# Counting the softmax sums out of bounds inside layer 1 of the last feed-forward group, with one relu of that layer put behind two PSUM copies of layer 2

## Chip, cores and metric

The kernel runs on one core of one Trainium2 chip. The metric is the device time of one execution in microseconds (us), here given as the median of several runs. Names used for the engines: PE or TensorE (matmuls; PEld is its loading of weights), DVE or VectorE, ACT or ScalarE, POOL or GpSimd, SP or SyncE (issues DMAs).

## The reference, cut to what matters

Attention over 8 batches and 8 heads (1152 keys, head size 64) with pairs of queries averaged, so that 576 rows of 512 values come out for each batch. Then a "mixture of depths": in each batch the 128 rows with the highest gate score go through a two-layer feed-forward network; the rest are passed on unchanged. All is float32.

```
    q_pool = q.reshape(B, H, S // factor, factor, D).mean(axis=3)
    scores = scale * np.matmul(q_pool, k.transpose(0, 1, 3, 2))
    scores = scores - np.max(scores, axis=-1, keepdims=True)
    attn = np.exp(scores)
    attn = attn / (np.sum(attn, axis=-1, keepdims=True) + 1e-09)
    return np.matmul(attn, v).astype(np.float32)
...
    scores = np.einsum('bsd,d->bs', x, w_gate)
    out = x.copy()
    for b in range(B):
        top_idx = np.argpartition(-scores[b], capacity)[:capacity]
        xe = x[b, top_idx]
        h = np.maximum(xe @ w1, 0.0)
        ye = h @ w2
        g = 1.0 / (1.0 + np.exp(-scores[b, top_idx]))
        out[b, top_idx] = x[b, top_idx] + g[:, None] * ye
```

w1 is 512 x 1024, w2 is 1024 x 512, and the capacity is 128.

## The kernel before, in words

**Attention.** `run` goes through 32 pairs of heads in halves. Of each half, TensorE makes the scores (L878), ScalarE their exponentials (L885) without the subtraction of a maximum, TensorE the product with the values (L896). Because no maximum is taken off, the kernel keeps all sums of exponentials in a tile `sums` (128 x 576) and at the end counts how many lie within fixed bounds (0.05 and 1e12). If any lies outside, a branch at the end of the program (label "again") computes everything anew in another way; with these inputs it isn't taken.

**Routing.** `routed` ranks the gate scores of a batch, fetches the chosen 128 rows with an indirect DMA (the tile `xe`, for the last batch a slice of a `v_sb` tile), and turns them for TensorE.

**Feed-forward.** The chosen rows are handled in two groups of four batches, in `ending`, after the attention. A matrix product is cut into quarters and made from seven products of quarters or of sums of quarters instead of eight (Strassen's scheme in Winograd's form). Sums of inputs come from `four_sums` (VectorE, L1410) or `input_sums` (GpSimd, L1256). Layer 1 of the second group (batches 4 to 7) is the generator `layer` within `split`. Of its seven products, four are whole (`first_product`, L1330, 16 matmul records each) and three are cut into seven smaller ones again (`inner_layer`, its matmuls at L1296, its first copy at L1308, its six other PSUM readers being VectorE sums at L1357, one product being read by two of them). `layer` ends each piece with a `yield`: 1 the product of a11 and b11; 2 an inner layer, the sum `rest(c11, u)` and `relu(c11)`; 3 the product of s2 and t2; 4 an inner layer; 5 the product of s1 and t1; 6 an inner layer, a sum for layer 2, and `rest(u, c22)` with its relu; 7 the product of s3 and t3, which two VectorE sums read, `relu(c22)`, three sums for layer 2, and last `rest(c21, v)` and `relu(c21)`. A `rest` is a VectorE sum of 128 x 1024 (L1357), a `relu` a ScalarE activation (L1490).

Layer 2 works on two batches at a time. Batches 4 and 5 use c11 and u (c12), batches 6 and 7 use c21 and c22. `second_of` makes the seven products of the first of these two in the order 1, 5, 2, 7, 3, 4, 6 (`second_product`, L1344, 8 matmul records each). ScalarE copies products 1, 5 and 3 out of PSUM (L1420, L1422, L1429), VectorE adds the others (L1357), scales by the gate and adds the row itself (`scaled`, L1352). The products of batches 6 and 7 are written out at the end of `ending` (copies at L1616 and L1618). Then four indirect scatters on GpSimd's queue (`written`, L1240) put the rows into the output in device memory.

**The count.** `counted` (L1644) reads `sums` twice on VectorE with an accumulated result, each pass followed by a read of the accumulator; `outside` adds over the partitions with a small matmul into a PSUM buffer (L1659), copies it (L1661), adds the two values (L1663) and turns them into an integer `count_i` (L1665). `values_load` (L1612) then loads that integer into a register on all five engines, with a branch hint (L1823), ahead of the branch (L1793).

**What sets the order.** The program is written in the order in which every engine's queue gets its instructions; nothing is reordered by a scheduler. `pieces(unit, n)` runs n pieces of a generator, and between them pieces of the routing (`waiting`) and of the weights' sums. Waits between engines follow from the tiles. The PSUM pool has four buffers of two banks, taken in turn by `banks()`: a product has to wait until the one four turns before it has been read.

Of the kernel before, what the change touches and what calls it, by code (L numbers as in the profile page):

```python
# [540 lines left out]
class _Plain:  # L541
# [814 lines left out]
    def add(self, to, x, y):  # L1356
        self.nc.vector.tensor_tensor(out=to, in0=x, in1=y, op=ALU.add)  # L1357
# [83 lines left out]
    def ending(self, halves, old):  # L1441
# [7 lines left out]
        def pieces(unit, n=None, of=1):  # L1449
            nonlocal done  # L1450
            for i, _ in enumerate(unit):
                for _ in range(of):
                    if done in behind:
                        next(waiting)
                    for _ in range(2):
                        next(weights, None)
                    done += 1
                if i + 1 == n:
                    break
# [10 lines left out]
        def halves_of(turned):  # L1470
            k = self.ND // 2
            return turned[:, :, 0:k, 0:w], turned[:, :, k:, 0:w]

        def first():
            a = [half_of for token in self.tokens[0 : self.B // 2 : 2] for half_of in halves_of(token["turned"])]
            c = [self.hidden_of(rooms[0][:, k * n : (k + 1) * n], w) for k in range(4)]
            m = [self.hidden_of(room[:, 4 * n : 5 * n], w) for room in rooms]
            return a, c, self.first_layer(a, inputs, c, m)

        def lines(room):  # L1480
            return self.lines_of(room)[:, :, 0:w]

        def across(room):
            return room.rearrange("p (t f) n -> p f t n", t=2)

        def rest(to, x):
            self.add(to, to, x)

        def relu(to):
            nc.scalar.activation(to, to, AF.Relu)  # L1490

        def split(a):
            u, v = (lines(room[:, 4 * n : 5 * n]) for room in rooms)
            c11, c21, c22 = (lines(rooms[1][:, k * n : (k + 1) * n]) for k in (0, 2, 3))
            c = [c11, u, c21, c22]
            temps = [
                [lines(rooms[0][:, k : k + half]) for k in range(2 * n + 3 * i * half, 2 * n + 3 * (i + 1) * half, half)]
                for i in range(2)
            ]
            two, six, seven = operands  # L1500
            s1, s2, s3, s4 = inputs
            t1, t2, t3, _ = (self.summed(1, i) for i in range(4))
            x, product, add = second(1, 0, c), self.first_product, self.add

            def layer():
                copy(across(u), product(a[0], self.quarter(1, 0, 0)))
                yield
                self.inner_layer(two, c11, temps[0])
                rest(c11, u)
                relu(c11)  # L1510
                yield
                add(across(v), across(u), product(s2, t2))
                yield
                self.inner_layer(seven, c21, temps[1])
                yield
                add(across(c22), across(v), product(s1, t1))
                yield
                self.inner_layer(six, u, temps[0])
                self.four_sums(*x[1:], slice(2, 3))
                rest(u, c22)  # L1520
                relu(u)
                yield
                ps = product(s3, t3)
                add(across(c22), across(c22), ps)
                add(across(v), across(v), ps)
                relu(c22)
                self.four_sums(*x[1:], slice(0, 2))
                self.four_sums(*x[1:], slice(3, 4))
                rest(c21, v)
                relu(c21)  # L1530
                yield

            return c, x, layer()

        def second(i, j, c):
            if i == 0:
                a = [c[2 * j + k][:, :, t, :] for t in range(2) for k in range(2)]
            else:
                a = [c[2 * j + k][:, 4 * t : 4 * t + 4, :] for t in range(2) for k in range(2)]
            s = self.lines_in(rooms[1 - i][:, 2 * j * n : 2 * (j + 1) * n], self.NFC // 2, w, 4)  # L1540
            return self.tokens[4 * i + 2 * j : 4 * i + 2 * j + 2], a, s
# [13 lines left out]
        a, c, layer = first()  # L1555
# [21 lines left out]
        x, y = second(0, 0, c), second(0, 1, c)  # L1577
        self.four_sums(*x[1:])
        pieces(layer, of=2)
        layer = self.second_of(*x, acc[1])  # L1580
# [3 lines left out]
        a = [half_of for token in self.tokens[self.B // 2 :: 2] for half_of in halves_of(token["turned"])]  # L1584
# [7 lines left out]
        self.input_sums(a, inputs, slice(3, 4))  # L1592
        self.inner_inputs(operands[1])
        self.input_sums(a, inputs, slice(2, 3))
        c, x, layer = split(a)
        pieces(layer)
        self.scattered(y[0])
        y = second(1, 1, c)
        layer = self.second_of(*x, acc[1])
        pieces(layer, 3)  # L1600
        low = self.counted()
        pieces(layer, 1)
        self.four_sums(*y[1:])
        pieces(layer, 1)
        outside = self.outside(low)
        pieces(layer)
        self.scattered(x[0])

# [218 lines left out]
```

## Time and profile before

| what | value |
|---|---|
| median of 3 runs | 674.19 us (674.08 to 674.79) |
| the profiled execution's own time | 673.19 us |
| its span, first to last instruction | 671.5 us |
| TensorE busy | 664.0 us, 99% of the span |
| mean granted TensorE clock | 0.997 |
| layer 1 of the second group begins on TensorE | 616.70 us (first whole product) |
| layer 2 of batches 4 and 5 begins | 639.92 us |
| the count's matmul (L1659) | 649.60 us |
| last scatter issued (L1240) | 666.65 us |

All times within the trace are counted from the start of the span. A row of the timeline gives the start, the time from the first start to the last end of a merged group, engine, line, operation, written and read tiles, shapes and number, and in brackets the idle time of the engine before it and what is thought to have ended it. Matmuls overlap, so the starts of following groups say more of TensorE's pace than their lengths do. A row of the table of stretches gives the length, then each engine's busy time and number of instructions.

### The profile page before, as it was taken

The numbers are of one execution on the slowest core, as the hardware profiler recorded it, in microseconds if no ns is written. First come the engines' busy times: TensorE is split into PE (matmuls) and PEld (weight loads), VectorE is DVE, ScalarE is ACT, GpSimd is POOL, SyncE is SP. The second block draws the span as 40 slices with busy tenths as digits, with TensorE's granted clock in tenths as the row PEclk, the third lists the DMA queues.
The fourth block names the chain that finished last, engine by engine and source line by source line (L and its number), as shares of the span: only waits on it lengthen the run. The fifth ranks groups of instructions, "written<-read, shape, count | busy, mean of one in ns | idle before, by whom it ended". The sixth has DMA issues, their size and how long they took to land.

```text
span 671.5 us, 23013 instructions
## 1 busy us (share of the span) xinstructions
PE 664.0 (99%) x9751; PEld 438.1 (65%) x9751; DVE 576.4 (86%) x832; ACT 441.3 (66%) x959; POOL 515.9 (77%) x489
## 2 busy tenths in 40 slices
PE   9999999999999999999999999999999999999996
PEld 6656666666666666666666666656666666888975
DVE  3878998998999987999899889988898898597783
ACT  6677778777777777777777777777777874221120
POOL 5788888889888988889888978898889877804502
PEclk9999999999999999999999999999999999999998
DMA  8988989858886788758976978588858745302001
GB/s 166 168 176 188 203 187 197 159 103 180 158 155 117 127 166 176 140 102 176 172 122 125 171 137 150 128 160 153 147 124 157 148 139 150 75 37 83 32 2 67
DMA packets 391048, 92.68 MB, mean 138 GB/s; under 512 B 371608, under 2 KB 376088, under 8 KB 390936
## 3 DMA queue, kind: packets, MB, share of 16 engines
q1 hardware_dynamic: 389496, 86.73, 66.7%
q0 software_dynamic: 1280, 4.20, 1.7%
q8 instruction: 78, 1.28, 0.8%
q14 instruction: 34, 0.28, 0.2%
q10 hardware_dynamic: 160, 0.20, 0.1%
HBM read 75.30 MB, written 15.79 MB: 136 GB/s over the span
## 4 chain that ended last, share of the span: by engine, by line
PE 97%; DMA 1%; DVE 1%; ACT 0%; issue 0%; POOL 0%; POOLq 0%
PE ps L878 42%; PE ps L896 42%; PE ps L1330 6%; PE ps L1344 5%; PE ps L1296 1%; PE ps L623 1%; DVE p L1357 1%; DMA out_dram<-xe,index 0%; DMA out_dram<-v_sb,index 0%; DVE p L1410 0%; ACT p L1490 0%; POOL out_dram L1240 0%; PE ps L844 0%; PE ps L830 0%; ACT acc L1429 0%
## 5 line engine op out<-in xcount | busy, mean ns | idle before, releaser
L885 ACT ACTIVATE p<-ps 128x576 f32<-128x576 f32 x576 | 320.5, 698 | 2.1 <-PE ps L878 1.9
L917 POOL TENSOR_TENSOR acc<-p 128x576 f32<-128x576 f32 x192 | 282.8, 1500 | 37.7 <-ACT p L885 36.9
L878 PE MATMUL ps<-qT,kT 64*64 64x288 f32 x4608 | 291.8, 403 | 0.1
L896 PE MATMUL ps<-p,v_sb 64*64 64x288 f32 x4608 | 290.9, 403 | 0.0
L878 PEld LDWEIGHTS ps<-qT,kT 64*64 64x64 f32 x4608 | 174.1, 133 | 105.3 <-ACT p L885 13.5
L896 PEld LDWEIGHTS ps<-p,v_sb 64*64 64x64 f32 x4608 | 172.8, 133 | 106.8 <-ACT p L885 14.7
L922 DVE TRANSPOSE_TENSOR_REDUCE fold<-p 128x54 f32<-128x1728 f32 x64 | 126.3, 1973 | 41.6 <-ACT p L885 41.4
L904 ACT COPY two<-ps 128x576 f32<-128x576 f32 x64 | 40.9, 638 | 133.2 <-PE ps L896 131.3
L922 DVE TRANSPOSE_TENSOR_REDUCE fold<-acc 128x54 f32<-128x1728 f32 x64 | 124.5, 1945 | 4.1 <-POOL acc L917 3.9
L906 POOL TENSOR_TENSOR av<-two 128x288 f32<-128x288 f32 x64 | 51.3, 801 | 39.8 <-ACT two L904 39.0
L766 DVE STREAM_TRANSPOSE kT<-kb 128x1152 f32<-128x1152 f32 x31 | 74.2, 2393 | 0.0
L985 POOL TENSOR_TENSOR prod<-avb,w_gate 128x288 f32<-128x288 f32 x64 | 51.5, 805 | 0.0
L763 POOL TENSOR_TENSOR qp<-qb 128x576 f32<-128x576 f32 (+1 forms) x32 | 43.8, 1370 | 5.8 <-DMA qb<-in_q_dram 4.3
L1116 DVE TENSOR_SCALAR_CACHE_REDUCE pick<-line 128x127 f32<-128x127 f32 (+4 forms) x80 | 45.2, 564 | 3.2 <-DMA line<-gate_lines 0.9
L962 ACT ACTIVATE sums<-total,tiny 32x18 f32<-32x18 f32 x124 | 38.2, 308 | 1.9
L1021 POOL TENSOR_TENSOR x<-avb,rec 128x576 f32<-128x576 f32 x30 | 34.8, 1159 | 0.0
L1240 POOL DMA_INDIRECT out_dram<-xe,index x7 | 7.1, 1011 | 33.3 <-DVE xe L1352 24.6
L975 DVE STREAM_TRANSPOSE avb<-av 128x288 f32<-128x288 f32 x64 | 28.3, 442 | 3.5 <-POOL av L906 3.5
L1043 DVE TENSOR_REDUCE red<-prod 128x9 f32<-128x288 f32 x64 | 27.8, 435 | 2.8 <-POOL prod L985 2.8
L947 ACT COPY groups<-sum 32x36 f32<-32x36 f32 x124 | 27.2, 219 | 1.6
L1357 DVE TENSOR_TENSOR p<-p,ps 128x256 f32<-128x256 f32 (+1 forms) x32 | 20.5, 690 | 8.8 <-PE ps L1330 6.5
L932 DVE TENSOR_REDUCE sum<-fold 128x18 f32<-128x108 f32 x64 | 21.7, 340 | 2.2
(148 smaller groups left out, 436.7 us busy)
## 6 DMA issues: line engine op xcount, KB each, us to landing
kb<-in_k_dram SPq DMA_DIRECT2D x124, 144.0 KB, 4.4
qb<-in_q_dram SPq DMA_DIRECT2D x124, 144.0 KB, 4.5
v_sb<-in_v_dram SPq DMA_DIRECT2D x31, 576.0 KB, 4.7
out_dram<-x SPq DMA_DIRECT2D x128, 72.0 KB, 4.7
lines<-row_rank SPq DMA_DIRECT2D x8, 640.0 KB, 4.9
w<-in_moe_w_dram SPq DMA_DIRECT2D x8, 512.0 KB, 5.4
line<-gate_lines SPq DMA_DIRECT2D x8, 351.5 KB
tw<-tw SPq DMA_DIRECT2D x4, 512.0 KB, 5.7
```

Source lines behind the costliest of these rows:

```text
L763: nc.gpsimd.tensor_tensor(out=qp[:, of, :], in0=pair["q"][:, of, 0, :], in1=pair["q"][:, of, 1, :], op=ALU.add)
L766: nc.vector.transpose(kT.rearrange("p (c i g) -> p c g i", c=self.NC, i=BLK), pair["k"].rearrange("p (g c) d -> p c g d", c=self.NC),)
L878: nc.tensor.matmul(sc[keys, j, 0:n], lhsT=pair["kT"][rows, c * P + keys.start : c * P + keys.stop], rhs=pair["qT"][rows, qs], start=True, ...
L885: nc.scalar.activation(p[:, c // G, c % G, :, :], sc[:, :, 0:n], AF.Exp, scale=self.scale)
L896: nc.tensor.matmul(av[j * self.D : (j + 1) * self.D, e, 0:n], lhsT=half["pair"]["v"][keys, j, c, :], rhs=half["p"][keys, c // G, c % G, j, :],
L904: nc.scalar.copy(two[:, :, :], av[:, :, 0:n])
L906: nc.gpsimd.tensor_tensor(out=half["av"][:, :], in0=two[:, 0, :], in1=two[:, 1, :], op=ALU.add)
L917: nc.gpsimd.tensor_tensor(out=acc[:, u, :], in0=units[:, 0, u, :], in1=units[:, 1, u, :], op=ALU.add)
L922: nc.vector.tensor_reduce(fold[:, a, :], of.rearrange("p u (m d) -> p (u m) d", d=BLK), AX.X, ALU.add, apply_transpose=True,)
L985: self.nc.gpsimd.tensor_tensor(out=pair["prod"][:, ns, :], in0=pair["avb"][:, ns, :], in1=self.w_gate[:, hp : hp + 1, :].broadcast_to([P, ...
L1116: nc.vector.tensor_scalar(out=cmp[0:rows, 0 : part.stop - part.start], in0=near[0:rows, part], scalar1=sc[0:rows, t : t + 1], scalar2=None ...
L1330: self.nc.tensor.matmul(to[:, f], lhsT=by[:, k, f * P : (f + 1) * P], rhs=of[:, :, k, :], start=k == 0, stop=k == n - 1,)
```

## The change

The sum `rest(c21, v)` and `relu(c21)` are taken out of the generator of layer 1 into a function `last_hidden`, which is called after the first two pieces of layer 2 of batches 4 and 5. `counted` is called after piece 4 of layer 1 instead of after the third product of layer 2, and `outside` after piece 6 of layer 1 instead of after the fifth product of layer 2. Four pieces of layer 2 come before the sums for batches 6 and 7, as before. The functions `counted` and `outside` themselves are the same, and what is computed is the same.

```
@@ split @@
                 relu(c22)
                 self.four_sums(*x[1:], slice(0, 2))
                 self.four_sums(*x[1:], slice(3, 4))
+                yield
+
+            def last_hidden():
                 rest(c21, v)
                 relu(c21)
-                yield
-
-            return c, x, layer()
+
+            return c, x, layer(), last_hidden
@@ ending @@
-        c, x, layer = split(a)
+        c, x, layer, last_hidden = split(a)
+        pieces(layer, 4)
+        low = self.counted()
+        pieces(layer, 2)
+        outside = self.outside(low)
         pieces(layer)
         self.scattered(y[0])
         y = second(1, 1, c)
         layer = self.second_of(*x, acc[1])
-        pieces(layer, 3)
-        low = self.counted()
-        pieces(layer, 1)
+        pieces(layer, 2)
+        last_hidden()
+        pieces(layer, 2)
         self.four_sums(*y[1:])
-        pieces(layer, 1)
-        outside = self.outside(low)
         pieces(layer)
         self.scattered(x[0])
```

The two functions that are moved:

```
    def counted(self):
        nc, n = self.nc, self.B * self.NPAIR * self.QB
        low = self.small.tile([P, 2], F32, name="low")
        flags = self.ffn.tile([P, n], F32, name="pick", bufs=1)
        for i, (op, bound) in enumerate(((ALU.is_ge, self.LO), (ALU.is_le, self.HI))):
            nc.vector.tensor_scalar(
                out=flags[:, :],
                in0=self.sums.rearrange("p a n -> p (a n)"),
                scalar1=bound,
                scalar2=None,
                op0=op,
                op1=ALU.add,
                accum_out=low[:, i : i + 1],
            )
        return low

    def outside(self, low):
        nc, n = self.nc, self.B * self.NPAIR * self.QB
        ps = self.banks()[:, 0, :]
        nc.tensor.matmul(ps[0:1, 0:2], lhsT=self.ones[:, 0:1], rhs=low[:, :], start=True, stop=True)
        found = self.small.tile([1, 2], F32, name="found")
        nc.vector.tensor_copy(found[:, :], ps[0:1, 0:2])
...
```

## The prediction

> **What bounds the kernel now.** I read the engine shares first, then the chain of waits, the table of stretches, the waits of that stretch and the timeline.
>
> ```profile
> PE 664.0 (99%) x9751; PEld 438.1 (65%) x9751; DVE 576.4 (86%) x832; ACT 441.3 (66%) x959; POOL 515.9 (77%) x489
> ...
> PE 97%; DMA 1%; DVE 1%; ACT 0%; issue 0%; POOL 0%; POOLq 0%
> ```
> TensorE is busy 99% of the span and carries 97% of the chain: only idle TensorE time, or the tail behind it, can move the end.
>
> ```profile
> core 0: us, PE busy (x) PEld busy (x) DVE busy (x) ACT busy (x) POOL busy (x), PEclk, DMA share, GB/s
> 620.15:636.47 16.32, 16.32 (x118) 15.49 (x117) 11.14 (x22) 2.98 (x5) 10.92 (x14) 1.00 0.09 33
> ...
> 639.92:655.28 15.36, 14.73 (x68) 12.03 (x67) 13.33 (x27) 3.20 (x6) 0.00 (x0) 1.00 0.01 3
> 655.28:665.90 10.62, 10.52 (x49) 8.93 (x47) 5.16 (x13) 0.74 (x2) 2.94 (x3) 1.00 0.21 78
> ```
> Layer 1 of the last batches has no idle TensorE time (first row); the 15.36 us of the seven products of layer 2 of batches 4 and 5, with the count and the first product of 6 and 7, have 0.63 us of it (second row). VectorE has 5.2 us to spare in layer 1 and 2.0 in the second stretch: the count sits where VectorE is fullest.
>
> ```profile
> 644.45 1.22 DVE L1357 TENSOR_TENSOR p<-p 128x1024 f32<-128x1024 f32 x1
> 645.70 1.06 ACT L1490 ACTIVATE p<-p 128x1024 f32<-128x1024 f32 x1 [3.26 <-DVE p L1357]
> 646.66 0.35 ACT L1420 COPY acc<-ps 128x256 f32<-128x256 f32 x1
> 647.07 1.99 PE L1344 MATMUL ps<-kb,p 128*128 128x256 f32 x8
> ...
> 649.37 0.08 DVE L1644 DVE_READ_ACCUMULATOR pick<-sums 128x1 f32 x1
> 649.60 0.19 PE L1659 MATMUL ps<-low,ones 128*1 128x2 f32 x2 [0.54 <-ACT acc L1429]
> 649.72 1.99 PE L1344 MATMUL ps<-qb,p 128*128 128x256 f32 x8
> 652.59 0.14 DVE L1665 TENSOR_SCALAR count_i<-count 1x1 int32<-1x1 f32 x1
> 653.44 1.59 PEld L1344 LDWEIGHTS ps<-w,p 128*128 128x128 f32 x8 [0.41 <-issue]
> ```
> Three stalls. (1) The product at 647.07 follows those at 639.92, 641.65, 643.38 and 645.10, 1.727 us apart. There are four PSUM buffers; the fifth product needs the buffer of the first, emptied by the ScalarE copy at 646.66, which stands behind the relu at 645.70, which waits for the last sum of layer 1 (644.45). (2) The count's matmul at 649.60: the page blames the copy of L1429, but the count's own accumulator read also ends at 649.45. (3) TensorE loads count_i into a register when VectorE has made it (652.73); the load runs 652.77 to 653.26, the branch hint to 653.40, and TensorE has run dry.
>
> **What the Trainium skill says.** "TensorE: Matmul & The Clock Gate", section "Architectural detail", gives TensorE a queue of 64 entries. The trace agrees that its sequencer runs ahead: an event wait of L1344 shows at 636.65 with all 16 matmuls of the last L1330 product still ahead, and the final compare-branch at 661.77 with matmuls until 665.85. A register load that need not wait should thus be hidden. "Perfetto Trace Analysis", section "Identifying Dependency Chains", says an instruction that waits for several engines may get event-semaphore instructions in front of it. The trace shows them, 0.05 us each. "SBUF — State Buffer", section "SBUF: two separate sides", says VectorE with two SBUF inputs and GpSimd lock each other out of a shared port pair. The trace fits: the same 128x1024 sum took 2.19 us at 624.31 beside GpSimd sums, 1.22 otherwise. Each count pass has one SBUF input tensor.
>
> **What the edit really moves.** In the compiled order, VectorE's last sum of layer 1 keeps its place; only its ScalarE relu goes behind the two copies. The two count passes go to after the second inner layer's sums, the count's matmul to before the last L1330 product (s3 t3), its three small VectorE operations to before that product's first sum. GpSimd's and SP's orders are unchanged; no DMA moves.
>
> **Removed from TensorE**, between 639.92 and 655.28 (three decimals: the start of a single matmul in the same timeline).
>
> - Stall 1: 647.066 - (645.102 + 1.727) = 0.237, plus a slow restart: the next matmul starts 0.320 after the first instead of 0.216, so 0.104. The copies will follow their products (about 642.7 and 644), buffers are free some 3 us early. The relu is not needed before the sums for batches 6 and 7; it ends at about 647.2, their first product comes after 652. Cost zero; cover 5 us.
> - Stall 2: the previous product's next matmul was due at 648.897, so 0.703 of waiting, 0.119 for the matmul itself, 0.104 of restart.
> - Stall 3: due 653.277, came 653.456: 0.179, plus 0.094 of restart. count_i will be ready at about 640 and the load runs ahead. Here it is bounded from 0 to the old 0.27; I take 0.
>
> Sum 0.237 + 0.104 + 0.703 + 0.119 + 0.104 + 0.179 + 0.094 = 1.540 us. Second way: 15.356 - 8 x 1.727 = 1.54.
>
> **Added.** The count passes take 647.90 to 649.45, 1.55 us, with 1.66 to the end of their overhead. They start at 630.70, when the seven sums of the second inner layer end, in this idle time:
>
> ```profile
> 633.54 3.73 DVE L1357 TENSOR_TENSOR p<-p,ps 128x1024 f32<-128x1024 f32 x8 [2.85 <-PE ps L1330]
> 640.12 2.35 DVE L1357 TENSOR_TENSOR p<-p,ps 128x1024 f32<-128x1024 f32 x2 [1.11 <-PE ps L1330]
> ```
> 2.85 us of cover leaves 1.2 in hand; without it the 1.66 would delay every later sum of layer 1. The three small operations (652.24 to 652.66, 0.42) fall into the 1.11 us before 640.12. The sums have been final since 573. Cost zero both times.
>
> The matmul is the part that costs. It takes the next of the four PSUM buffers, so the turn of each later product shifts by one: s3 t3, which began at 636.47, now needs the buffer of the third inner layer's fifth product rather than its fourth. That one is read by two sums, and the second ends at 636.20 + 0.415 = 636.62; the event wait at 636.65 above is this release, as yet needed by the next product only, three us later. Counting from it as the old count matmul did from its own wait (649.492 to 649.600, 0.108): the product starts at 636.76 instead of 636.47, 0.29, and with a restart of 0.10 TensorE is **0.40** late; the matmul's 0.12 lies inside it. Bounds: 0.12 if nothing waits, 0.45 if the sums slip by one event wait (0.05).
>
> Net on TensorE: 1.540 - 0.40 = **1.14 us**. Queued behind the new wait are layer 2's matmuls alone; what s3 t3 feeds slips by 0.40 on VectorE, which then has no count, so the sums needed by 652.4 end at about 650.3.
>
> **Does the end follow?** Behind 655.28 the products follow 1.727 apart, so TensorE is the limit there. The four scatters go one by one, each also waiting for the landing of the one before:
>
> ```profile
> 655.63 0.98 POOL L1240 DMA_INDIRECT out_dram<-xe,index  x1 [22.07 <-DVE xe L1352]
> 659.22 0.98 POOL L1240 DMA_INDIRECT out_dram<-xe,index  x1 [2.61 <-DMA out_dram<-xe,index]
> 663.15 0.98 POOL L1240 DMA_INDIRECT out_dram<-v_sb,index  x1 [2.95 <-DVE v_sb L1352]
> 666.65 0.98 POOL L1240 DMA_INDIRECT out_dram<-xe,index  x1 [2.52 <-DVE xe L1352]
> ```
> The third waits for v_sb (662.87; the landing came at 662.30), the fourth for xe (666.32; landing 665.88). Both VectorE ends follow TensorE by 1.14. The first scatter comes about 1.8 earlier, as VectorE no longer lags, so the second lands at about 660.5, before the 661.7 that the third needs. The last 4.9 us (scatter, landing, closing waits) stay. So the end follows whole.
>
> The sum is made against the profiled execution, 673.19 us with a span of 671.5: 672.05. It was 1.00 under the median 674.19; carried over, 674.19 - 1.14 = **673.05**, 0.17% faster. About 0.2% (1.35 us) is what a measurement of this kernel can tell from no change.
>
> **Rivals.**
>
> - *The insertion is almost free* (0.40): s3 t3's buffer comes in time, or the restart costs nothing because queued weights are loaded already. TensorE pays 0.12, gain 1.42, **672.77**. For it: weight loads overlap matmuls throughout. Against: the event wait at 636.65.
> - *A wait takes the place of those removed* (0.10): the register load still drains TensorE (0.27), or a buffer waits again. Gain 0.87 or less, **673.32**. Against: the compare-branch four us ahead.
> - *Slower* (0.05): the count overruns VectorE's idle time, because GpSimd's two scatter issues (629.57, 632.58) or its port hold it. It would delay the sum at 633.54, all seven behind it, and s3 t3's buffer. Slowed like the sum at 624.31 (2.19/1.22 = 1.8) it takes 3.0 us and costs 0.15. It decides only beyond 2.85 + 1.14 = 4.0 us; at three times its length (5.0) it overruns by 2.1 and the kernel ends at **675.0**. Against: at 629 to 633 GpSimd runs no sums.
>
> **How the numbers follow.** The forecast as worked out has 0.45 (own range 672.8 to 673.4). Faster by over 0.2% takes the almost-free case and the forecast's lower edge, 0.40 + 0.03; within 0.2% takes the rest of the forecast and the second rival, 0.42 + 0.10; slower 0.05. The range goes from 672.3 (all 1.54 gained) to 673.7 (the second rival), each widened by 0.35, half the 0.71 between the runs shown.
>
> **What would show it.** Right: the products of layer 2 start 1.727 apart without idle time; the copies of L1420 and L1422 precede the last relu; the count lies within VectorE's idle time before 633.54; the stretch of 15.36 us shrinks to 13.8; s3 t3 starts at about 636.76. Wrong: s3 t3 at 636.6 (first rival), idle TensorE time around the register load (second), the sum of 633.54 late (third), or a last scatter that waits for a landing.

## The result, and the profile after

The changed kernel took 672.57 us, the median of 17 runs (672.25 to 674.42), against 674.17 us of the kernel before in 17 runs beside it: ratio 0.9977, 95% interval 0.9969 to 0.9984. In a second comparison it took 672.18 against 673.52 us, ratio 0.9982 (0.9975 to 0.9989). The forecast was 673.05 against 674.19, a ratio of 0.9983, which lies in both intervals. The first median lies 0.48 us below the forecast time. Which side of the 0.2% line the kernel is on, these runs don't settle.

The traces are more exact than the medians, if one leaves out what comes before the edit: two traces of each kernel agree to 0.01 us there (e4 and e10 below). The profiled execution after took 672.48 us with a span of 670.7 (before: 673.19 and 671.5), but it reached the edited part 0.44 us *later*. So I measure from a point just ahead of the edit: from the first matmul of the s1 t1 product (L1330) to the first matmul of the last pair of layer 2 products. It is called **the stretch** below. Before, it is 662.18 - 629.89 = 32.30 us (worked out from unrounded starts), as the timeline of TensorE shows (start, length of the merged group, engine, line):

```profile
629.89 3.62 PE L1330 MATMUL ps<-acc,tw 128*128 128x256 f32 x16
...
636.47 3.62 PE L1330 MATMUL ps<-acc,tw 128*128 128x256 f32 x16
...
662.18 3.62 PE L1344 MATMUL ps<-w,p 128*128 128x256 f32 x16
```

After:

```profile
630.32 3.62 PE L1330 MATMUL ps<-acc,tw 128*128 128x256 f32 x16
...
636.46 0.61 PE L1296 MATMUL ps<-kT,prod 128*128 128x128 f32 x4
637.00 0.19 PE L1663 MATMUL ps<-low,ones 128*1 128x2 f32 x2
637.20 3.69 PE L1330 MATMUL ps<-acc,tw 128*128 128x256 f32 x16
640.72 1.89 PE L1344 MATMUL ps<-w,p 128*128 128x256 f32 x8
642.45 1.89 PE L1344 MATMUL ps<-kb,p 128*128 128x256 f32 x8
644.18 1.89 PE L1344 MATMUL ps<-w,p 128*128 128x256 f32 x8
645.90 1.89 PE L1344 MATMUL ps<-kT,p 128*128 128x256 f32 x8
647.63 1.89 PE L1344 MATMUL ps<-kb,p 128*128 128x256 f32 x8
649.36 1.89 PE L1344 MATMUL ps<-qb,p 128*128 128x256 f32 x8
651.08 3.62 PE L1344 MATMUL ps<-w,p 128*128 128x256 f32 x16
...
661.44 3.62 PE L1344 MATMUL ps<-w,p 128*128 128x256 f32 x16
```

From 640.72 on the products start 1.727 us apart without a break, where before they broke at 647.07, 649.60 and 653.46. The seven products with the first of batches 6 and 7 take 654.54 - 640.72 = 13.82 us instead of 15.36. The stretch is 661.44 - 630.32 = 31.12 us, 1.17 less. The last scatter starts 35.59 us after the beginning of the stretch instead of 36.76, also 1.17 less: the end follows. The table of stretches, over the same times as before (639.92 to 655.28), now reads

```profile
639.92:655.28 15.36, 15.36 (x73) 13.53 (x72) 12.60 (x22) 4.11 (x7) 0.98 (x1) 1.00 0.01 3
```

with TensorE busy all the 15.36 us. What made room is seen on VectorE and ScalarE:

```profile
631.05 0.74 DVE L1648 TENSOR_SCALAR_CACHE_REDUCE pick<-sums 128x576 f32<-128x576 f32 x1
...
632.51 0.08 DVE L1648 DVE_READ_ACCUMULATOR pick<-sums 128x1 f32 x1
633.98 3.73 DVE L1357 TENSOR_TENSOR p<-p,ps 128x1024 f32<-128x1024 f32 x8 [1.38 <-PE ps L1330]
...
639.72 0.14 DVE L1669 TENSOR_SCALAR count_i<-count 1x1 int32<-1x1 f32 x1
640.92 2.35 DVE L1357 TENSOR_TENSOR p<-p,ps 128x1024 f32<-128x1024 f32 x2 [1.06 <-PE ps L1330]
```

```profile
643.14 0.35 ACT L1420 COPY acc<-ps 128x256 f32<-128x256 f32 x1
644.38 0.37 ACT L1422 COPY acc<-ps 128x256 f32<-128x256 f32 x1 [0.88 <-PE ps L1344]
646.50 1.06 ACT L1490 ACTIVATE p<-p 128x1024 f32<-128x1024 f32 x1 [1.75 <-DVE p L1357]
```

The count lies within idle time (1.38 us are left of 2.85), and the two copies, counted from the beginning of the stretch, are made 4.0 and 3.0 us earlier, ahead of the relu.

### The profile page after: what moved, and what is told of

It reads as the page before. It is cut to its first block, busy times and chain, and to the rows that moved or that the text cites. A ratio compares the mean times of both kernels' runs of the same rounds, so it can differ in the third digit from the quotient of the medians.

```text
span 670.7 us, 23013 instructions
## 1 busy us (share of the span) xinstructions
PE 663.9 (99%) x9751; PEld 438.9 (65%) x9751; DVE 573.9 (86%) x832; ACT 441.0 (66%) x959; POOL 515.8 (77%) x489
## 4 chain that ended last, share of the span: by engine, by line
PE 92%; issue 4%; DMA 2%; POOL 2%; DVE 1%; POOLq 0%; DVEq 0%
PE ps L878 42%; PE ps L896 42%; PE ps L1330 4%; PE ps L1344 3%; DMA out_dram<-xe,index 1%; PE ps L623 1%; POOL acc L1256 1%; POOL p L1256 1%; DMA out_dram<-v_sb,index 0%; DVE acc L1357 0%; POOL out_dram L1240 0%; PE ps L844 0%; DVE xe L1352 0%; POOL kT L1256 0%; DVE v_sb L1215 0%
```

## The experiments

All ratios are to the kernel before, run beside each kernel. The last columns are from each kernel's trace: the stretch, and the gain in it against 32.30.

| kernel | ratio (95% interval) | stretch, us | gain, us |
|---|---|---|---|
| changed | 0.9977 (0.9969 to 0.9984) | 31.12 | 1.17 |
| e1, relu alone moved | 0.9983 (0.9976 to 0.9989) | 31.07 | 1.22 |
| e2, count alone moved | 0.9991 (0.9982 to 0.9999) | 31.47 | 0.83 |
| e3, matmul behind s3 t3 | 0.9982 (0.9976 to 0.9989) | 31.07 | 1.22 |
| e4, before again | 0.9999 (0.9991 to 1.0007) | 32.30 | -0.01 |
| e5, count's end behind the last scatter | 1.0016 (1.0010 to 1.0023) | 30.76 | 1.54 |
| e6, four passes, early place | 0.9985 (0.9978 to 0.9991) | 31.25 | 1.05 |
| e7, four passes, late place | 1.0003 (0.9995 to 1.0012) | 32.42 | -0.13 |
| e8, integer made late | 1.0004 (0.9995 to 1.0013) | 32.43 | -0.13 |
| e9, no matmul for the count | 0.9975 (0.9964 to 0.9985) | 30.76 | 1.54 |
| e10, changed again | 0.9982 (0.9975 to 0.9989) | 31.12 | 1.17 |

### Which part brings the gain: e1 and e2

e1 keeps the count where it was and moves only the relu (and the sum ahead of it, whose place in VectorE's queue is the same). `split` is as in the change; in `ending`, against the kernel before:

```
         layer = self.second_of(*x, acc[1])
-        pieces(layer, 3)
+        pieces(layer, 2)
+        last_hidden()
+        pieces(layer, 1)
         low = self.counted()
```

> The kernel before with the relu and last sum of layer 1 put behind the two copies, the count left where it was. I measure TensorE from the first matmul of the s1 t1 product (629.89 in the profile of before) to the first matmul of the last pair of layer 2 products (662.18): 32.29 us before, 31.12 after. Theory A (one queue of lateness): the relu was the root; without it VectorE's sum of the second copy starts at about 645.6 instead of 647.04, the count is done at about 648.0, before TensorE gets to its matmul, and count_i is ready at about 651.3, before TensorE has run dry; so all three stalls go, less about 0.32 for the count's matmul and its restart: 31.07 us, ratio about 0.9982. Theory B (each part has its own stall): the relu is worth only the first stall, 0.34: 31.95 us, ratio about 0.9995.

e2 is the changed kernel with `last_hidden()` called at the end of layer 1 again:

```
                 self.four_sums(*x[1:], slice(3, 4))
+                last_hidden()
                 yield
...
-        pieces(layer, 2)
-        last_hidden()
-        pieces(layer, 2)
+        pieces(layer, 4)
```

> The changed kernel with the relu and last sum back at the end of layer 1: only the count is moved. Same measure of TensorE (32.29 before, 31.12 after). Theory A: the first stall stays (the fifth product of layer 2 waits for the copy of the first, about 0.23 and a restart of 0.10), the other two go, the new wait at s3 t3 (0.37) comes: 32.29 - 1.20 + 0.37 = 31.46, ratio about 0.9988. Theory B gives the same number, since it adds the parts; the two differ in the sum of both runs' gains (A 2.0 us, B 1.17).

Measured: 31.07 for e1 and 31.47 for e2. The relu alone brings 1.22 us, all that the whole change brings and slightly more; the count alone brings 0.83. Together they would be 2.05 if parts added; the change brings 1.17. Theory A, in which lateness is handed on, holds. The sum that reads the first copy, in the kernel before:

```profile
647.04 0.42 DVE L1357 TENSOR_TENSOR acc<-acc,ps 128x256 f32<-128x256 f32 x1 [1.38 <-ACT acc L1420]
```

VectorE, then TensorE with the table of stretches, of e1:

```profile
646.09 0.41 DVE L1357 TENSOR_TENSOR acc<-acc,ps 128x256 f32<-128x256 f32 x1
...
648.40 0.08 DVE L1648 DVE_READ_ACCUMULATOR pick<-sums 128x1 f32 x1
...
651.62 0.14 DVE L1669 TENSOR_SCALAR count_i<-count 1x1 int32<-1x1 f32 x1
```

```profile
630.39 3.62 PE L1330 MATMUL ps<-acc,tw 128*128 128x256 f32 x16
...
647.33 1.89 PE L1344 MATMUL ps<-kb,p 128*128 128x256 f32 x8
649.15 0.19 PE L1663 MATMUL ps<-low,ones 128*1 128x2 f32 x2
649.27 1.99 PE L1344 MATMUL ps<-qb,p 128*128 128x256 f32 x8
651.11 3.62 PE L1344 MATMUL ps<-w,p 128*128 128x256 f32 x16
...
661.47 3.62 PE L1344 MATMUL ps<-w,p 128*128 128x256 f32 x16
```

```profile
639.92:655.28 15.36, 15.36 (x74) 13.24 (x73) 14.18 (x29) 4.18 (x7) 0.61 (x1) 1.00 0.01 3
```

The count is unmoved, yet it is ready (648.48) before TensorE comes to its matmul (649.15), and the integer is there at 651.76, 1.1 us before the next product is due at 652.84. The sum that reads the first copy (646.09) starts directly behind its predecessor; in the kernel before VectorE sat idle for 1.38 us ahead of it, waiting for the copy of L1420. So all three stalls of the kernel before had one root, whose lateness was handed on: relu, copy (stall 1), VectorE's sum, count, matmul (stall 2), integer (stall 3). That VectorE is full is not the reason: in e1 it is busy 14.18 of these 15.36 us, in the kernel before 13.33, and yet TensorE never waits.

### What the inserted matmul costs: e3

```
-        pieces(layer, 2)
+        pieces(layer, 3)
         outside = self.outside(low)
```

> The changed kernel with the count's matmul behind the s3 t3 product instead of ahead of it. Theory A (the turn of the PSUM buffers makes s3 t3 wait for a buffer that two sums read): s3 t3 takes its old buffer and starts right behind the inner layer; the matmul costs about 0.2 to 0.3 with its own restart ahead of layer 2: 31.12 - 0.1 = 31.0 us on the same measure, and no event wait of L1330 at the s3 t3 product. Rival (the small matmul itself stops the pipeline wherever it stands): the whole 0.37 moves with it, 31.12. In time, both are within 0.02% of the changed kernel.

Measured: s3 t3 starts 6.58 us into the stretch as in the kernel before (6.87 in the changed kernel), directly behind the inner layer, and the stretch is 31.07. The event wait of s3 t3 (L1330) passes 0.67 us ahead of its first matmul, at 636.12; in the changed kernel it passes at 637.09, and s3 t3 starts 0.11 us after it. So the turn of the buffers is real, but the matmul costs 0.32 of the 0.37 us here too, where no buffer is late: both theories hold a part. TensorE of e3:

```profile
636.79 3.62 PE L1330 MATMUL ps<-acc,tw 128*128 128x256 f32 x16
640.34 0.19 PE L1663 MATMUL ps<-low,ones 128*1 128x2 f32 x2
640.46 1.99 PE L1344 MATMUL ps<-w,p 128*128 128x256 f32 x8
642.29 1.89 PE L1344 MATMUL ps<-kb,p 128*128 128x256 f32 x8
```

In single rows: the last matmul ahead makes room after 0.216, the small one starts 0.310 after it (0.094 late), takes 0.119, and the matmul behind it takes 0.320 instead of 0.216. Sum 0.094 + 0.119 + 0.104 = 0.317.

### Does the count need its early place: e6 and e7

Both make four passes instead of two, of which the first two are for nothing; e6 on the changed kernel, e7 on e1. The matmul reads the last two counts alone, as before.

```
-        low = self.small.tile([P, 2], F32, name="low")
+        low = self.small.tile([P, 4], F32, name="low")
...
-        for i, (op, bound) in enumerate(((ALU.is_ge, self.LO), (ALU.is_le, self.HI))):
+        for i, (op, bound) in list(enumerate(((ALU.is_ge, self.LO), (ALU.is_le, self.HI)) * 2))[::-1]:
```

> The changed kernel with four count passes instead of two (two of them for nothing). Four passes take about 3.15 us, and VectorE's idle time there is 2.93 us: they overrun by 0.2 to 0.3, which delays the sums of the third inner layer and with them s3 t3. Theory A: 31.12 + 0.25 = 31.4 us on the same measure, ratio about 0.9986; the first idle 2.85 us are free, what lies above counts in full. Rival (the count costs nothing there because VectorE has 14% to spare): 31.12.

> The kernel with the relu alone moved, with four count passes instead of two. The count then ends at about 650.06 instead of 648.49, and TensorE comes to its matmul at 649.15. Theory A: the late place has about 0.6 us in hand, so 1.57 more delay the matmul by 1.05 and the register load adds about 0.3: 31.07 + 1.35 = 32.4 us, ratio about 1.000; the early place of the count is worth something only when VectorE is late. Rival (the place of the count never matters): 31.07.

Measured: e6 31.25, e7 32.42. VectorE of e6:

```profile
633.86 0.08 DVE L1648 DVE_READ_ACCUMULATOR pick<-sums 128x1 f32 x1
633.86 3.73 DVE L1357 TENSOR_TENSOR p<-p,ps 128x1024 f32<-128x1024 f32 x8
```

The sum of s1 t1 has lost its bracket: it no longer waits for TensorE but for the count. It starts 3.79 us into the stretch instead of 3.66, and s3 t3 and the end of the stretch are late by the same 0.12 to 0.13. I had expected 0.25; 0.08 of the difference is that I let the sum wait for the end of the last accumulator read, and it starts beside it (both at 633.86). So the overrun counts in full and the idle time ahead of it is free; the rival "free because VectorE has time to spare" falls. TensorE of e7:

```profile
651.05 0.19 PE L1663 MATMUL ps<-low,ones 128*1 128x2 f32 x2 [1.00 <-DVE pick L1648]
```

The releaser is now the count itself. 1.57 us more of VectorE delay TensorE by 1.07 at this matmul and by another 0.28 at the load, as both come later than in e1. So the early place is worth nothing to the kernel as it is (e1 is as good as the changed one), but has about 1.4 us in hand (1.57 - 0.12) against some 0.5 in the late one (1.57 - 1.07).

### What a late integer costs: e8

`outside` is split (left out here); the sum of the two values and the integer come behind the sums of product 4 of layer 2, the sixth made.

```
         self.four_sums(*y[1:])
+        pieces(layer, 2)
+        outside = self.outside_count(outside)
         pieces(layer)
```

> The changed kernel with the last two operations of the count (sum of the two values and integer) behind the sums of the fourth product of layer 2, so that count_i is ready about 23.1 us after the start of s1 t1 instead of 9.5. Theory A (the load stops TensorE when the integer is late): TensorE needs the next product at 22.49, the load and hint end about 0.65 after count_i, so the product comes about 1.3 late with 0.1 of restart: 31.12 + 1.4 = 32.5 us, ratio about 1.000. Rival (the 0.27 us at the load in the kernel before was the branch hint, not the wait): no change, 31.12.

Measured: 32.43, 1.31 more than the changed kernel (expected 1.4). All engines and weight loads of e8, and below TensorE's load of the register (a q marks an engine's sequencer, which works through the engine's queue; durations in ns):

```profile
653.11 0.14 DVE L1676 TENSOR_SCALAR count_i<-count 1x1 int32<-1x1 f32 x1
...
654.08 1.59 PEld L1344 LDWEIGHTS ps<-w,p 128*128 128x128 f32 x8 [1.44 <-issue]
654.11 1.96 PE L1344 MATMUL ps<-w,p 128*128 128x256 f32 x8 [1.07 <-DVE xe L1352]
```

```profile
L1618 PEldq TENSOR_LOAD <-count_i x1: 492/492/492, 653.3 to 653.3; - x1
```

From the end of the integer (653.25) to the next matmul pass 0.86 us; the load starts 0.04 us after the integer is made, and takes 0.49 of them. The releaser in brackets, a VectorE scaling, is not needed by this matmul; the sequencer stood at the register load. Where count_i is early, as in the changed kernel, the load runs at 648.95, 3.9 us before the product behind it is due, and costs nothing.

### Getting rid of the matmul: e5 and e9

e5 takes matmul, small operations, load and hint out of their places (left out here) and puts them behind the last scatter:

```
         self.written(six, six["index"])
+        outside = self.outside(low)
+        found = nc.values_load(outside[0:1, 0:1])
+        E = mybir.EngineType
+        self.tc.mark_branch_hint_location("again", found, [E.PE, E.DVE, E.Pool, E.Activation, E.SP])
         return found
```

> The changed kernel with the count's matmul, its three small operations, the register load and the branch hint behind the last scatter; the two count passes stay where the change put them. Theory A: the matmul costs TensorE about 0.3 us wherever it stands between products, so without it the stretch from the first matmul of s1 t1 to the first of the last pair is 32.30 - 1.54 = 30.76 us (31.12 in the changed kernel), and the load and the branch fit beside the landing of the last scatter (about 2.8 us): the end comes 0.36 us earlier than in the changed kernel, ratio to before about 0.9977. Rival: load and jump at the end aren't hidden and cost 0.5 to 3 us there: ratio 0.999 to 1.003.

Measured: the stretch is 30.76 as expected and the last scatter 0.37 us earlier than in the changed kernel, but the end comes 42.78 us after the beginning of the stretch instead of 40.41, and the ratio is 1.0016 (1.0010 to 1.0023). The rival holds, and most of the time is lost at the branch (durations in ns):

```profile
L1797 PEldq COMPARE_BRANCH  x1: 4215/4215/4215, 666.3 to 666.3; - x1
L1797 ACTq EVENT_SEMAPHORE  x1: 17/17/17, 669.7 to 669.7; - x1
L1797 PEldq EVENT_SEMAPHORE  x1: 51/51/51, 670.6 to 670.6; - x1
L1797 POOLq EVENT_SEMAPHORE  x1: 17/17/17, 670.8 to 670.8; - x1
```

All five engines reach their branch at 666.2 to 666.3, some 0.1 us after their hints, and run their next instruction 3.5 to 4.6 us later. On GpSimd the 2.38 us can be followed whole. Its branch comes 36.00 us into the stretch instead of 35.37, 0.63 later, as load and hint now come behind the scatter's start; its next instruction follows 4.47 us after the branch instead of 2.72, 1.74 more; and from there to the last instruction both kernels take 2.32 us. Why the wait behind the branch is longer is not shown: all five engines branch at once and right after their hints, and beside it the last scatter lands 4.93 us after its start instead of 2.75.

e9 takes the sum over partitions off TensorE and leaves the rest of the changed kernel as it is (the values lie in columns added to the flags' tile; these lines, and a VectorE memset of 0.09 us that zeroes a part of them, are left out below):

```
+        for g in range(P // BLK):
+            nc.scalar.copy(self.four[:, g, :], low[g * BLK : (g + 1) * BLK, :])
         return low
...
-        nc.tensor.matmul(ps[0:1, 0:2], lhsT=self.ones[:, 0:1], rhs=low[:, :], start=True, stop=True)
-        found = self.small.tile([1, 2], F32, name="found")
-        nc.vector.tensor_copy(found[:, :], ps[0:1, 0:2])
-        count = self.small.tile([1, 1], F32, name="count")
-        nc.vector.tensor_reduce(count[:, :], found[:, :], AX.X, ALU.add)
+        nc.vector.tensor_reduce(
+            self.column[:, 0:1], self.four.rearrange("p g a -> p (g a)"), AX.X, ALU.add
+        )
...
+        nc.vector.tensor_reduce(
+            count[:, :],
+            self.column.rearrange("p (n d) -> p n d", d=BLK),
+            AX.X,
+            ALU.add,
+            apply_transpose=True,
+        )
...
```

> The changed kernel with the sum over partitions taken off TensorE: four small ScalarE copies put the counts of the four groups of 32 partitions side by side, and two small VectorE operations add them up; load, hint and branch stay where the change has them. Theory A: the 0.37 us that the change still loses at the count's matmul goes and nothing new waits, since ScalarE is idle from 628 to 634 and VectorE has 1.1 us before the sums of s3 t3: 30.76 us from the first matmul of s1 t1 to that of the last pair (31.12 in the changed kernel), the end 0.37 us earlier than the changed kernel, ratio to before about 0.9977. Rival: the copies or sums delay a ScalarE or VectorE step that TensorE waits for: 31.1 or more.

Measured: 30.76, the end 40.06 us after the beginning of the stretch (40.41 in the changed kernel), and 671.79 us (671.30 to 672.09) against 673.52, ratio 0.9975 (0.9964 to 0.9985). Beside it on the same chip the changed kernel took 672.18: e9 is the fastest of all kernels here by its trace; in time the two intervals overlap. TensorE, ScalarE and VectorE of e9:

```profile
630.09 3.62 PE L1330 MATMUL ps<-acc,tw 128*128 128x256 f32 x16
...
660.84 3.62 PE L1344 MATMUL ps<-w,p 128*128 128x256 f32 x16
```

```profile
632.41 0.80 ACT L1662 COPY pick<-low 32x2 f32<-32x2 f32 x4 [4.35 <-DVE pick L1652]
```

```profile
639.31 0.20 DVE L1672 TRANSPOSE_TENSOR_REDUCE pick<-pick 32x1 f32<-32x32 f32 x1
639.54 0.14 DVE L1680 TENSOR_SCALAR count_i<-pick 1x1 int32<-1x1 f32 x1
640.32 2.35 DVE L1357 TENSOR_TENSOR p<-p,ps 128x1024 f32<-128x1024 f32 x2 [0.64 <-PE ps L1330]
```

### Where the 1.6 us of the first comparison come from: e4 and e10

> The kernel before once more, for a second profile of it. Theory A: the stalls of layer 2 are the same to 0.05 us (32.29 on the same measure), because they follow from fixed instruction times; then the difference between the gain in the traces (1.17) and in the medians (1.6) comes from elsewhere or from noise. Rival: in an execution near the median (674.2, where the one profiled first took 673.19) one of the stalls is up to 0.5 us longer.

> The changed kernel once more, beside the one without the matmul. Theory A: 31.12 us on the same measure and 1.17 us under the kernel before, ratio 0.9983; the first comparison's 1.6 us was 1.17 and noise. Rival: 1.6 us again (ratio 0.9976), and then some 0.4 us of the gain lies outside what the traces show.

Measured: the stretch is 32.30 and 31.12, each the same as in the first profile to 0.01 us. Second medians: 672.18 for the changed kernel, 1.34 under the one before. 1.17 lies in both intervals; that the first comparison's other 0.4 us are noise is the simplest reading, not shown beyond that.

## Why the prediction was right, and where its reasons were not

**Size and place of the gain.** Predicted 1.540 - 0.40 = 1.14 us; the trace has 1.17. The removed 1.540 is confirmed by e9 and e5, whose stretch is 32.30 - 30.76 = 1.54.

**The added 0.40.** Measured 0.366: s3 t3 begins 0.293 later (predicted 0.29) and its first step is 0.073 longer (predicted 0.10). The buffer's release did end last, as predicted. But the prediction had the matmul "lie inside" that wait, and so made the wait the price; e3 shows that matmul and restart cost 0.32 without it, and the wait adds 0.05. In the changed kernel's own rows the 0.366 is a late start of the small matmul (0.094, which the prediction had not seen), its own step (0.119), the rest of the wait (0.080) and the longer first step (0.073). The first rival ("almost free", 0.12) falls at the three places tried: ahead of s3 t3, ahead of layer 2 (e3) and within layer 2 (e1).

**The three stalls as three causes.** Here the prediction's reasoning failed, though its sum did not: it assigned stall 1 to the relu and stalls 2 and 3 to the place of the count. e1 removes all three by moving the relu alone. The count stood where VectorE was fullest, as the prediction said, but it was late only because VectorE had waited 1.38 us for a ScalarE copy just ahead of it. The bracket `[1.38 <-ACT acc L1420]` in the timeline of before says so; I had not used it. That the forecast held all the same is luck in this one respect: the change moves both parts, so how the 1.54 us divide between them didn't matter. For the relu alone the same prices give 0.34 us, and e1 measured 1.22.

**Cover.** 2.85 us of idle VectorE time for the count: right, and e6 shows that it ends there; the count took 1.47 of them (1.38 are left), not 1.66. The register load hidden by the run-ahead: right (load at 648.95, product due at 652.81), and e8 shows the price without it. The relu's cover: it ends at 647.56, VectorE's first sum that reads it starts at 648.23, right behind the operation before it, and the product that needs these sums is due at 652.81; nothing waits for it.

**The tail.** The last scatter came 1.17 us earlier within the stretch's frame, as TensorE did; its wait was VectorE's, as forecast. The last scatter and what follows it kept their length (4.80 us before, 4.82 after), but what sets the end there is a branch and not the landing (last section). The slower rival (overrun of the count) did not happen: the passes took 1.54 us and fell between GpSimd's two scatter issues (630.01 to 631.00 and 633.02 to 634.00). In e6 two passes ran beside the second issue (632.77 to 633.75), and took 0.75 us each like the others. That rival's own sum was off: an overrun of 2.1 us gives 674.19 - 1.14 + 2.1 = 675.2, not 675.0.

## What to carry to other kernels

When an engine in strict order shows several stalls in a row, look for the first and ask which of the later ones it feeds, before giving each a price of its own: their gains do not add. An engine's copy out of PSUM should not stand behind an operation that waits for a busy third engine and whose result is needed only later. A tiny matmul between full ones costs TensorE some 0.3 us in this kernel, so a sum over partitions that isn't urgent may be cheaper on engines with idle time.

## What the hardware showed that I had not expected

- A matmul of 128 x 1 weights with 2 columns cost 0.32 us among matmuls of 0.216 us pace (e1, e3), only 0.12 of it its own step.
- After a compare-branch the next instruction of the same engine came 2.5 to 2.9 us later in the changed kernel on SyncE, ScalarE, VectorE and GpSimd, whether its hint was 11 us old (VectorE) or 0.1 (SyncE). On TensorE it came after 4.07 us, at the end of its matmuls. When all five engines branched right after their hints (e5), it was 3.5 to 4.6 us.
- GpSimd's branch sets the end. In the changed kernel its branch is at 665.69 and its next instruction at 668.41; a drain of 1.38 us ends at 669.89, when SyncE has been through its waits for the landings since 669.30.

```profile
L1797 POOLq COMPARE_BRANCH  x1: 73/73/73, 665.7 to 665.7; - x1
...
L1797 POOLq EVENT_SEMAPHORE  x1: 17/17/17, 668.4 to 668.4; - x1
```

In all twelve traces the last instruction ends 2.32 us after this instruction of GpSimd, while it ends 1.98 to 2.63 us after the landing of the last scatter; in all but e5 the instruction comes 0.18 to 0.34 us ahead of that landing, so it doesn't wait for it. Without this branch SyncE's waits would come last in the changed kernel; the gain from that, an estimate from the figures above, would be some 0.6 us at most (669.89 - 669.30). No kernel here tried that.
